# The second inverse step of a Fourier filter: three products in one PSUM bank

## The chip, the cores and the metric

The kernel runs on one core of a Trainium2 chip. The metric is the device time of one execution in microseconds (us). A core has TensorE (matrix products, which land in PSUM, here 8 banks of 128 partitions by 512 float32 columns), VectorE, ScalarE and GpSimd (elementwise work), and SyncE, whose queue issues most DMA transfers. In profile rows they are PE (PEld for its weight loads), DVE, ACT, POOL and SP. No GpSimd operation of this kernel touches PSUM.

## The reference

A signal `x` of 8 batches by 3008 positions by 256 channels is filtered in the frequency domain along its positions, and every position's 256 results then go through an MLP with a Gelu in its sigmoid form:

```
X = np.fft.rfft(x, axis=1)
y = np.fft.irfft(X * (filt_r + 1j * filt_i), n=3008, axis=1)
h = y.reshape(24064, 256) @ w_in          # 256 -> 2048
out = (h / (1 + np.exp(-1.702 * h))) @ w_out   # 2048 -> 256
```

All arrays are float32.

## The kernel before

**The transform.** 3008 = 64 x 47, so the transform of a batch is a 64-point one (first step), then a 47-point one (second forward step), the product with the filter, the 47-point inverse (second inverse step) and the 64-point inverse (first inverse step). Each is a matrix product with a table. The 64 frequencies of the first step are handled in 16 groups; a group has real and imaginary parts of two frequencies by 256 channels. The 47 positions are folded into 48 rows (sums of cosines and of sines), so the tables of the second steps are 48 by 48.

**High and low parts.** TensorE's fast float32 form (float32r) keeps fewer bits, so a value is split: the high part is a copy in float32r, the low part is the value less its high part. A product of two values is then high x high + high x low + low x high; the fourth, low x low, is small.

**The second steps of batch 1 on** (`fft`, lines 673 to 788). In group `i`, `forward(i)` (746) has its data from DRAM in the buffer `zy`: partitions 0 to 47 hold the high parts, 64 to 111 the low parts, real and imaginary part side by side. `second` (735) issues two products of 112 rows by 512 columns, one for the real and one for the imaginary part, each into a PSUM bank of its own. Its table `de_sb` stacks the high table under both the high and the low rows, and the low table beside it in other columns; so 48 rows of the bank receive high table x (high + low), and 48 other rows low table x (high + low). `halves` (666) adds the two: for each bank ScalarE copies 48 rows out, and VectorE adds the other 48 rows to them. In group 0 each of the two products is done as two of 256 columns, since one frequency has another table. `product` (657) multiplies with the filter: three VectorE operations into `u_buf` and `c_buf`, and an add on GpSimd. Then the result, 112 partitions with the real part in 0 to 47 and the imaginary part in 64 to 111, is split for the inverse step: for each part VectorE casts the 48 high rows into `zy`, and GpSimd subtracts them for the 48 low rows, which are put at the other part's partitions. `backward(i)` (764) runs `second` and `halves` once more, with the inverse table and with a tile `raw` as the end, and every other group stores to DRAM (`b_d`), from where `pair_signal` loads it for the first inverse step.

**The MLP.** Batch 0 is transformed first and its MLP runs in plain form, while batch 1 is transformed beside it; this part is ordered by the tile framework. From batch 1 on the MLP takes tokens in pairs of tiles of 512 and hidden units in pairs of blocks, with seven products for eight (`product_of`, `gelu`, `second_of`): 168 cycles of 45 matmuls of 512 columns (448 in a batch's last tile), with some six VectorE additions and subtractions a cycle. Beside the cycles of batch `b` runs the transform of batch `b + 1`, for `b` from 1 to 6; beside those of batch 7 there is none.

**What sets the order.** In this second part all operations are first recorded by `Planner` (189 on) and not issued. `add` notes for each the operations it must follow, by the boxes of the tiles that it reads and writes; `price` gives it a cost; `dues` a due time, backwards from a timeline of TensorE's work; and `plan` places them on the engines one after another, the most urgent first. It takes VectorE operations without PSUM and GpSimd operations one at a time. The order it finds is the order in which each engine executes: on every engine an operation waits until all those written ahead of it have started. `fft` is a generator, taken further by `advance` (1108) as the MLP's products are recorded: a transform's second steps are spread over the stretch that the MLP leaves. Banks of PSUM are given out by the planner as well: four (`bank_h`) serve the MLP's first products and the transform together, four (`bank_o`) the MLP's results.

The planner issues everything at one line, so in profile rows the planned part stands under L393, and the first part under L406. There operations are told apart by the tiles that they write and read. `bank_h<-zy,de_sb` are the products of both second steps, `raw<-bank_h,raw` of 48 partitions is the add of `halves` in the inverse step, and `c_buf<-bank_h,c_buf` is that in the forward step. Buffers of one pool can carry several names: `c_f` is the sum that feeds one of the MLP's four Gelus.

Of the kernel before, what the change touches and what calls it, by code (L numbers as in the profile page):

```python
# [9 lines left out]
F32 = mybir.dt.float32  # L10
# [4 lines left out]
ALU = mybir.AluOpType  # L15
# [170 lines left out]
class Planner:  # L186
# [56 lines left out]
    def add(self, eng, call, args, kw):  # L243
        o = Op()
        o.eng, o.call, o.args, o.kw = eng, call, args, kw
        aps = [a for a in (*args, *kw.values()) if isinstance(a, (bass.AP, View))]
        o.cost, o.extra, o.port = self.price(eng, call, args, aps)
        o.preds, o.succs, o.opens = set(), [], []
        o.names = {a.tensor.name: a.tensor for a in aps}
        n = len(self.ops)  # L250
        self.ops.append(o)
        for i, a in enumerate(aps):
            name, box, writes = a.tensor.name, self.box(a), i == 0
            if name not in self.seen:
                self.seen[name] = []
                if isinstance(a, View):
                    o.opens.append(a.tensor)
            kept = []
            for m, b, w in self.seen[name]:
                meets = b[0] < box[1] and box[0] < b[1] and b[2] < box[3] and box[2] < b[3]  # L260
                if meets and (w or writes) and m != n:
                    o.preds.add(m)
                inside = box[0] <= b[0] and b[1] <= box[1] and box[2] <= b[2] and b[3] <= box[3]
                if not (writes and inside and m != n):
                    kept.append((m, b, w))
            kept.append((n, box, writes))
            self.seen[name] = kept
        for name in o.names:
            self.users.setdefault(name, []).append(n)
# [142 lines left out]
def tile_kernel(  # L412
# [27 lines left out]
    def held(name, tag="f", shape=(P, 2, D)):  # L440

        if nc.on:
            return nc.tile("h", shape, F32, name, tag)
        return ps_h.tile(list(shape), F32, tag="h", name=name)
# [10 lines left out]

    tab = const.tile([P, sum(WIDTHS.values())], F32, tag="tab", name="tab")
    t1_sb = const.tile([P, 2, P], F32R, name="t1_sb")
    de_sb = const.tile([Q, 2, 4, Q], F32R, name="de_sb")
    HALF = NFC // 2
    table, at = {}, 0  # L460
    for name, w in WIDTHS.items():
# [97 lines left out]
    def split_de():  # L559

        pin = tc.keep_in_program_order
        de_f = table["de"].rearrange("p (m c) -> p m c", m=4)
        pin(nc.scalar.copy(t1_sb[:, 0], table["t1"]))
        pin(nc.vector.tensor_tensor(t1_sb[:, 1], table["t1"], t1_sb[:, 0].bitcast(F32), ALU.subtract))
        pin(nc.gpsimd.memset(de_sb.bitcast(F32), 0.0))
        for k in range(2):
            h, o = slice(64 * k, 64 * k + 48), slice(64 - 64 * k, 112 - 64 * k)
            pin(nc.scalar.copy(de_sb[h, k, :, h], de_f[h, :, h]))  # L570
            pin(nc.vector.tensor_tensor(de_sb[h, k, :, o], de_f[h, :, h], de_sb[h, k, :, h].bitcast(F32), ALU.subtract))
            pin(nc.gpsimd.tensor_copy(de_sb[o, k], de_sb[h, k].bitcast(F32)))

    def first_fft():

# [87 lines left out]
        nc.vector.tensor_tensor(u1, xs[:Q], f_r, ALU.mult)  # L663
        nc.gpsimd.tensor_tensor(u1, u1, u2, ALU.add)

    def halves(ps, dst):

        for k in range(2):
            h, o = slice(64 * k, 64 * k + 48), slice(64 - 64 * k, 112 - 64 * k)
            nc.scalar.copy(dst[h], ps[k][o])  # L670
            nc.vector.tensor_tensor(dst[h], ps[k][h], dst[h], ALU.add)

    def fft(b):

        a_d = dram.tile([2, 48, 64, D], F32, tag="a_d", name=f"a_d{b}")
        store = nc.sync if nc.on else nc.scalar
        xrs, split = {}, {}

        def load_x(c):
            if c < 6:  # L680
                xrs[c] = raw(f"x_{b}_{c}", "x")
                load_in(xrs[c], x[b, c])

        def parts(n):
            if n < 12:
                c, u = divmod(n, 2)
                xh, xl = half(f"xh_{b}_{c}_{u}"), half(f"xl_{b}_{c}_{u}")
                src = xrs[c][:, 2 * u : 2 * u + 2, :]
                nc.scalar.copy(xh, src)
                nc.gpsimd.tensor_tensor(xl, src, xh.bitcast(F32), ALU.subtract)  # L690
                split[n] = xh, xl

        load_x(0)
        if nc.on:
            load_x(1)
            yield 4.0
            parts(0)
            yield 2.0
        for c in range(6):
            if nc.on:  # L700
                ah, al = (nc.tile("ab", (P, 4, D), F32R, f"a{n}_{b}_{c}") for n in "hl")
            else:
                ah, al = (sb.tile([P, 4, D], F32R, tag="raw", name=f"a{n}_{b}_{c}", bufs=7) for n in "hl")
            for u in range(2):
                parts(2 * c + u + nc.on)
                xh, xl = split.pop(2 * c + u)
                ps = held(f"s1_{b}_{c}_{u}")
                mm3(ps, t1_sb[:, 0], t1_sb[:, 1], xh, xl)
                su = slice(2 * u, 2 * u + 2)
                nc.scalar.copy(ah[:, su], ps)  # L710
                nc.vector.tensor_tensor(al[:, su], ps, ah[:, su].bitcast(F32), ALU.subtract)
                yield 1.5
            load_x(c + 1 + nc.on)
            for j in range(2):
                n = NH * j + 4 * c
                for k, a in enumerate((ah, al)):
                    store.dma_start(
                        a_d[k, n : n + 4].rearrange("n k d -> k n d"), a[64 * j : 64 * j + 64].bitcast(F32)
                    )

        b_d = dram.tile([48, 64, D], F32, tag="b_d", name=f"b_d{b}")

        def load(i):
            for k in range(2):
                src = a_d[k].rearrange("n (k s) d -> n k s d", k=2)[:, :, 2 * i : 2 * i + 2, :]
                (nc.sync if nc.on else nc.gpsimd).dma_start(
                    zy[0][64 * k : 64 * k + 48, i % 2].rearrange("p k s d -> p k (s d)").bitcast(F32 if nc.on else F32R),
                    src.rearrange("n k s d -> n k (s d)"),
                )

        def load_f(i):
            for k in range(2):
                load_in(f_buf[64 * k : 64 * k + 48, 2 * (i % 2) : 2 * (i % 2) + 2], fs[:, 2 * i : 2 * i + 2])

        def second(i, m, src, name):

            ps = [held(f"{name}_{b}_{i}_{k}") for k in range(2)]
            for k in range(2):
                if i == 0:
                    nc.tensor.matmul(ps[k][:Q, 0], de_sb[:, k, m + 1], src[:, k, 0], start=True, stop=True)  # L740
                    nc.tensor.matmul(ps[k][:Q, 1], de_sb[:, k, m], src[:, k, 1], start=True, stop=True)
                else:
                    nc.tensor.matmul(ps[k][:Q], de_sb[:, k, m], src[:, k], start=True, stop=True)
            return ps

        def forward(i):

            ps = second(i, 0, zy[0][:Q, i % 2], "s2")
            if i + 2 < 16:
                load(i + 2)  # L750
            u1 = c_buf[i % 3]
            halves(ps, u1)
            product(i, u1, u1, f_buf[:, 2 * (i % 2) : 2 * (i % 2) + 2])
            y = zy[0][:, 2 + i % 2]
            for k in range(2):
                h, o = slice(64 * k, 64 * k + 48), slice(64 - 64 * k, 112 - 64 * k)
                nc.vector.tensor_copy(y[h, k], u1[h])
                nc.gpsimd.tensor_tensor(y[o, k], u1[h], y[h, k].bitcast(F32), ALU.subtract)
            if i + 2 < 16:
                load_f(i + 2)  # L760

        bes = {}

        def backward(i):
            g, u = divmod(i, 2)
            if u == 0:
                bes[g] = raw(f"b_{b}_{g}", "ab")
            ps = second(i, 2, zy[0][:Q, 2 + i % 2], "i2")
            halves(ps, bes[g][:Q, 2 * u : 2 * u + 2, :])
            if u == 1:  # L770
                be = bes.pop(g)
                for k in range(2):
                    (nc.sync if nc.on else nc.scalar).dma_start(b_d[:, 32 * k + 4 * g : 32 * k + 4 * g + 4, :], be[64 * k : 64 * k + 48])

        for i in range(2):
            load(i)
            load_f(i)

        for i in range(2):
            yield 5.0  # L780
        for i in range(17):
            if i < 16:
                forward(i)
                yield 3.3
            if i:
                backward(i - 1)
                yield 3.3
        b_of[b] = b_d
# [425 lines left out]
```

## Time and profile before

| | us |
|---|---|
| median of 3 runs | 2452.57 (2451.43 to 2454.61) |
| profiled execution, its own time | 2448.9 |
| its span, first to last instruction | 2447.1 |
| mean granted TensorE clock | 0.989 of full |

The page of the profile gives each engine's busy time and share of the span, and then the chain of work that ended last. Views by stretch give, for each stretch of time, the busy us of every engine with its number of instructions. A matmul's end is modelled, and matmuls overlap: a row's mean of 390 ns for one of 512 columns is not the time between two. What an engine waited for is told by "[idle before <-releaser]": how long it stood still, and whose end let it go on.

### The profile page before, as it was taken

The page shows a single profiled execution, that of the slowest core. Times are in us where ns is not written, and L with a number is a line of the kernel's source. Part 1 is how long each engine was busy: PE and PEld are TensorE (multiplying, and loading weights), DVE is VectorE, ACT ScalarE, POOL GpSimd, SP SyncE. Part 2 cuts the span into 40 slices and gives each one's busy share as a digit, 9 for nine tenths or more (in the row PEclk, how much of TensorE's full clock was granted, in tenths as well). Part 3 has the DMA queues.
Part 4 walks back from the last instruction along what each step waited for, and adds up shares of the span by engine and source line. Part 5 has one row for each costly group of instructions (what it writes and reads, how often), then busy time and mean ns, then how long its engine had stood idle before and what let it go on. Part 6 is the DMA issues. An engine that isn't in the chain of part 4 may idle for free.

```text
span 2447.1 us, 32185 instructions
## 1 busy us (share of the span) xinstructions
PE 2333.3 (95%) x10578; PEld 1897.0 (78%) x10578; DVE 1751.6 (72%) x2603; ACT 1615.3 (66%) x2937; POOL 1105.8 (45%) x789
## 2 busy tenths in 40 slices
PE   8789889989999999999999999999999999999999
PEld 6667668868788787887778777887778887888887
DVE  6776996578965889559985588756997588854443
ACT  5555554767767677667676677666776777766665
POOL 4654662445534445345543445444553455532111
PEclk9899999999999999999999999999999999999999
DMA  9455443777769777697677976778776886754443
GB/s 290 145 155 141 111 131 119 253 222 213 220 190 294 217 209 214 199 300 210 195 218 224 266 214 198 215 253 233 216 219 199 263 245 204 214 186 154 153 159 120
DMA packets 199191, 500.48 MB, mean 205 GB/s; under 512 B 21488, under 2 KB 94448, under 8 KB 199024
## 3 DMA queue, kind: packets, MB, share of 16 engines
q1 hardware_dynamic: 187456, 481.90, 64.6%
q10 hardware_dynamic: 7984, 10.23, 1.5%
q0 software_dynamic: 3584, 6.29, 1.3%
q8 instruction: 84, 1.38, 0.2%
q14 instruction: 83, 0.68, 0.1%
HBM read 392.95 MB, written 105.38 MB: 204 GB/s over the span
## 4 chain that ended last, share of the span: by engine, by line
PE 76%; DVE 15%; DMA 3%; issue 2%; ACT 2%; POOL 1%; SPq 0%; ACTq 0%; DVEq 0%; POOLq 0%
PE bank_h L393 38%; PE bank_o L393 33%; PE h L406 2%; PE o L406 2%; DVE c_buf L393 1%; DVE u_buf L393 1%; DVE gl L406 1%; DVE wb L393 1%; DVE c_buf L406 1%; DVE u_buf L406 1%; DVE w_tu L406 1%; DVE bank_h L393 1%; DVE zy L393 1%; DVE ws L406 1%; DVE gl L393 1%
## 5 line engine op out<-in xcount | busy, mean ns | idle before, releaser
L393 PE MATMUL bank_o<-wc 128*128 128x512 f32 (+1 forms) x2016 | 553.8, 390 | 5.4 <-ACT wc L393 3.5
L393 PE MATMUL bank_h<-y_a,wa 128*128 128x512 f32 (+1 forms) x1584 | 434.9, 393 | 14.8 <-DVE c_f L393 8.8
L393 PEld LDWEIGHTS bank_o<-wc 128*128 128x128 f32 x2016 | 378.2, 189 | 91.0 <-ACT wc L393 10.6
L393 POOL TENSOR_TENSOR wc<-c_f,wc 128x512 fp32r<-128x512 f32 (+1 forms) x168 | 214.0, 1274 | 495.6 <-ACT c_f L393 366.5
L393 PE MATMUL bank_o<-gh,wc 128*128 128x512 f32 (+1 forms) x1344 | 390.2, 388 | 0.5 <-ACT gh L393 0.2
L393 PEld LDWEIGHTS bank_h<-y_a,wa 128*128 128x128 f32 x1584 | 294.0, 189 | 85.1 <-DVE c_f L393 11.8
L393 POOL TENSOR_TENSOR zy<-c_buf,zy 48x512 fp32r<-48x512 f32 x192 | 273.7, 1426 | 132.1 <-DVE zy L393 116.4
L393 DVE TENSOR_TENSOR gl<-bank_h,gh 128x512 fp32r<-128x512 f32 (+1 forms) x336 | 226.8, 677 | 114.5 <-ACT bank_h L393 109.4
L393 ACT ACTIVATE bank_h<-bank_h 128x512 f32<-128x512 f32 (+1 forms) x504 | 297.8, 591 | 0.0
L393 PEld LDWEIGHTS bank_o<-gh,wc 128*128 128x128 f32 x1344 | 251.8, 188 | 49.2 <-ACT gh L393 2.6
L393 ACT COPY wb<-bank_h 128x512 f32<-128x512 f32 (+1 forms) x309 | 178.6, 578 | 161.8 <-PE bank_h L393 159.3
L393 PE MATMUL bank_h<-y_bt,wa 128*128 128x512 f32 (+1 forms) x960 | 272.1, 393 | 13.3 <-DVE c_f L393 10.0
L393 POOL TENSOR_TENSOR c_buf<-c_buf,u_buf 112x512 f32<-112x512 f32 x96 | 125.1, 1303 | 285.4 <-DVE c_buf L393 273.1
L393 ACT ACTIVATE gh<-bank_h 128x512 fp32r<-128x512 f32 (+1 forms) x336 | 197.4, 588 | 67.2 <-DVE bank_h L393 37.6
L393 DVE TENSOR_TENSOR raw<-bank_h,raw 48x512 f32<-48x512 f32 (+1 forms) x264 | 180.8, 687 | 63.0 <-ACT raw L393 55.2
L393 DVE TENSOR_TENSOR bank_h<-bank_h,g 128x512 f32<-128x512 f32 x224 | 155.8, 696 | 93.3 <-PE bank_h L393 50.6
L393 PEld LDWEIGHTS bank_h<-y_bt,wa 128*128 128x128 f32 x960 | 177.9, 189 | 54.6 <-DVE c_f L393 13.5
L393 PE MATMUL bank_o<-gl,wc 128*128 128x512 f32 (+1 forms) x672 | 217.0, 387 | 0.0
L393 ACT COPY g<-bank_h 128x512 f32<-128x512 f32 x224 | 131.8, 588 | 111.0 <-PE bank_h L393 103.5
L393 DVE TENSOR_TENSOR wc<-bank_h,wc 128x512 fp32r<-128x512 f32 x168 | 115.7, 689 | 109.8 <-ACT bank_h L393 108.9
L393 DVE TENSOR_TENSOR c_f<-bank_h,wb 128x512 f32<-128x512 f32 (+1 forms) x168 | 112.2, 668 | 78.7 <-ACT wb L393 76.2
L393 PE MATMUL bank_h<-zy,de_sb 112*112 112x512 f32 (+1 forms) x408 | 154.6, 392 | 10.6 <-DVE wc L393 6.4
(166 smaller groups left out, 4154.5 us busy)
## 6 DMA issues: line engine op xcount, KB each, us to landing
wa<-w SPq DMA_DIRECT2D x168, 896.0 KB, 7.0
wc<-w SPq DMA_DIRECT2D x168, 512.0 KB, 4.3
f_buf<-fs SPq DMA_DIRECT2D x224, 192.0 KB, 3.9
a_d<-raw SPq DMA_DIRECT2D x144, 256.0 KB, 5.2
zy<-a_d SPq DMA_DIRECT2D x192, 192.0 KB, 4.3
out_dram<-out SPq DMA_DIRECT2D x40, 512.0 KB, 6.1
raw<-in_x_dram SPq DMA_DIRECT2D x36, 512.0 KB, 6.3
b_d<-raw SPq DMA_DIRECT2D x96, 192.0 KB, 3.9
```

Of the source, the lines that this page charges most:

```text
L393: getattr(getattr(self.nc, o.eng), o.call)(*map(real, o.args), **{k: real(v) for k, v in o.kw.items()})
L406: return real(*args, **kw)
```

## The change

The second inverse step of batches 1 to 7 is computed in another way. After the filter, VectorE casts all 112 rows into the first half of a `zy` buffer in one operation, and GpSimd subtracts all 112 rows for the low parts into the second half. The inverse table is a tile of its own, `e_sb`, with a high and a low part, each 112 by 112 with the real and the imaginary table on its diagonal. `backward` issues three products of 112 rows by 512 columns (high x high, high x low, low x high) which add up in one PSUM bank; in group 0 it is three for each of the two frequencies, of 256 columns. One ScalarE copy of 112 rows takes the sum to `raw`. The product of the low parts is no longer formed there. The forward step keeps its products and its `halves`, now written out inside `forward`, with a table `d_sb` half the size of `de_sb`. In the planner, a write of TensorE counts as one of the whole bank.

```
@@ Planner.add
+            if eng == "tensor" and writes:
+                box = (0, P, 0, 2048)
@@ tables
-    de_sb = const.tile([Q, 2, 4, Q], F32R, name="de_sb")
+    d_sb = const.tile([Q, 2, 2, Q], F32R, name="d_sb")
+    e_sb = const.tile([Q, 2, 2, Q], F32R, name="e_sb")
@@ split_de
-        pin(nc.gpsimd.memset(de_sb.bitcast(F32), 0.0))
+        pin(nc.scalar.copy(e_sb[:, 0], de_f[:Q, 2:4]))
+        pin(nc.vector.tensor_tensor(e_sb[:, 1], de_f[:Q, 2:4], e_sb[:, 0].bitcast(F32), ALU.subtract))
+        pin(nc.gpsimd.memset(d_sb.bitcast(F32), 0.0))
         for k in range(2):
...
@@ forward: the split for the inverse step
-            y = zy[0][:, 2 + i % 2]
-            for k in range(2):
-                h, o = slice(64 * k, 64 * k + 48), slice(64 - 64 * k, 112 - 64 * k)
-                nc.vector.tensor_copy(y[h, k], u1[h])
-                nc.gpsimd.tensor_tensor(y[o, k], u1[h], y[h, k].bitcast(F32), ALU.subtract)
+            y = zy[0][:Q, 2 + i % 2]
+            nc.vector.tensor_copy(y[:, 0], u1)
+            nc.gpsimd.tensor_tensor(y[:, 1], u1, y[:, 0].bitcast(F32), ALU.subtract)
@@ backward
-            ps = second(i, 2, zy[0][:Q, 2 + i % 2], "i2")
-            halves(ps, bes[g][:Q, 2 * u : 2 * u + 2, :])
+            ps, y = held(f"i2_{b}_{i}"), zy[0][:Q, 2 + i % 2]
+            for to, m, of in [(0, 1, 0), (1, 0, 1)] if i == 0 else [(slice(0, 2), 0, slice(0, 2))]:
+                for n, (wk, yk) in enumerate(((0, 0), (0, 1), (1, 0))):
+                    nc.tensor.matmul(ps[:Q, to], e_sb[:, wk, m], y[:, yk, of], start=n == 0, stop=n == 2)
+            nc.scalar.copy(bes[g][:Q, 2 * u : 2 * u + 2, :], ps[:Q])
```

## Rows read from the trace of the kernel before

**Rows 1.** The page, parts 1 and 4: engines' busy time; the chain that ended last.
```profile
PE 2333.3 (95%) x10578; PEld 1897.0 (78%) x10578; DVE 1751.6 (72%) x2603; ACT 1615.3 (66%) x2937; POOL 1105.8 (45%) x789
...
PE 76%; DVE 15%; DMA 3%; issue 2%; ACT 2%; POOL 1%; SPq 0%; ACTq 0%; DVEq 0%; POOLq 0%
```

**Rows 2.** Busy us (and instructions) by stretch: from:to, length, engines, clock, DMA; second-step stretches.
```profile
502.00:705.00 203.00, 193.17 (x840) 152.28 (x841) 170.18 (x257) 142.31 (x257) 97.91 (x71) 1.00 0.70 207
790.00:993.00 203.00, 193.37 (x850) 154.02 (x849) 170.34 (x257) 141.89 (x256) 100.33 (x71) 1.00 0.73 211
1082.00:1287.00 205.00, 195.71 (x854) 155.86 (x853) 170.75 (x257) 142.51 (x258) 100.83 (x71) 0.99 0.72 209
1376.00:1582.00 206.00, 196.76 (x852) 156.51 (x851) 170.71 (x257) 142.32 (x257) 100.72 (x71) 0.98 0.72 209
1671.00:1876.00 205.00, 195.79 (x853) 155.69 (x852) 170.58 (x257) 142.37 (x257) 100.73 (x71) 0.99 0.72 209
1953.00:2159.00 206.00, 203.02 (x906) 164.91 (x905) 173.39 (x269) 150.43 (x270) 104.58 (x74) 1.00 0.73 218
sum 1228.00, PE 1177.82 PEld 939.26 DVE 1025.95 ACT 861.83 POOL 605.10; mean PE 196.30 PEld 156.54 DVE 170.99 ACT 143.64 POOL 100.85
```

**Rows 3.** The same view, the sum of the five strips between those stretches.
```profile
sum 429.00, PE 428.29 PEld 364.26 DVE 231.43 ACT 297.64 POOL 186.85; mean PE 85.66 PEld 72.85 DVE 46.29 ACT 59.53 POOL 37.37
```

**Rows 4.** The same view: batch 1's second steps, and the MLP alone at the end.
```profile
150.00:420.00 270.00, 241.98 (x1078) 191.85 (x1078) 206.40 (x290) 142.86 (x262) 136.96 (x114) 0.99 0.50 138
2200.00:2400.00 200.00, 200.00 (x918) 167.56 (x918) 87.96 (x134) 121.95 (x221) 40.94 (x28) 1.00 0.44 157
```

**Rows 5.** TensorE's matmuls in order of time (start, us, operation): two runs of six.
```profile
2307.04 1.52 PE L393 MATMUL bank_h<-y_bt,wa 128*128 128x512 f32 x6
2308.40 1.52 PE L393 MATMUL bank_o<-wc 128*128 128x512 f32 x6
```

**Rows 6.** Waits of TensorE, its largest: us in total, times, longest.
```profile
PE bank_h L393 <- DVE c_f L393: 18.8, 12, 3.5
```

**Rows 7.** All engines in order of time, around TensorE's longest wait.
```profile
1398.45 3.20 POOL L393 TENSOR_TENSOR zy<-c_buf,zy 48x512 fp32r<-48x512 f32 x2 [1.07 <-DVE zy L393]
...
1398.86 1.67 DVE L393 SCALAR_TENSOR_TENSOR u_buf<-c_buf,f_buf 48x512 f32<-48x512 f32 x1
...
1400.56 1.64 DVE L393 TENSOR_TENSOR u_buf<-c_buf,f_buf 48x512 f32<-48x512 f32 x1
...
1403.58 1.65 PE L393 MATMUL bank_h<-y_bt,wa 128*128 128x512 f32 x3 [3.52 <-DVE c_f L393]
```

**Rows 8.** One tile's instructions, `u_buf`: ns shortest/median/longest, first and last start.
```profile
L393 DVE SCALAR_TENSOR_TENSOR u_buf<-c_buf,f_buf x96: 678/687/1719, 519.4 to 2139.7; 48x512 f32<-48x512 f32 x96
```

**Rows 9.** TensorE in order of time: a lone product of the second steps among others.
```profile
2101.68 0.40 PE L393 MATMUL bank_h<-zy,de_sb 112*112 112x512 f32 x1
2101.92 0.87 PE L393 MATMUL bank_o<-gh,wc 128*128 128x512 f32 x3
```

**Rows 10.** VectorE's groups, 500 to 2200 us: count, busy us, mean ns, idle before.
```profile
L393 DVE TENSOR_TENSOR raw<-bank_h,raw 48x512 f32<-48x512 f32 x192 | 131.7, 686 | 23.9 <-ACT raw L393 20.4 <-DMA f_buf<-fs 0.3
L393 DVE CAST zy<-c_buf 48x512 fp32r<-48x512 f32 x192 | 85.6, 446 | 4.6 <-POOL c_buf L393 1.1
...
L393 DVE TENSOR_TENSOR c_buf<-c_buf,f_buf 112x512 f32<-112x512 f32 x96 | 69.8, 727 | 2.6
```

**Rows 11.** GpSimd's groups of the second steps, the same stretch and columns.
```profile
L393 POOL TENSOR_TENSOR zy<-c_buf,zy 48x512 fp32r<-48x512 f32 x192 | 273.7, 1426 | 132.1 <-DVE zy L393 116.4 <-PE bank_h L393 7.3 <-PE bank_o L393 1.6
L393 POOL TENSOR_TENSOR c_buf<-c_buf,u_buf 112x512 f32<-112x512 f32 x96 | 125.1, 1303 | 285.4 <-DVE c_buf L393 273.1 <-PE bank_h L393 12.2
```

**Rows 12.** ScalarE's copies out of PSUM, the same stretch and columns.
```profile
L393 ACT COPY raw<-bank_h 48x512 f32<-48x512 f32 x192 | 111.7, 582 | 48.0 <-PE bank_h L393 42.3 <-DMA f_buf<-fs 1.0
...
L393 ACT COPY g<-bank_h 128x512 f32<-128x512 f32 x186 | 109.4, 588 | 97.0 <-PE bank_h L393 90.2 <-DVE c_buf L393 1.9 <-DVE bank_h L393 1.2
```

**Rows 13.** One tile's instructions, `de_sb`: its clearing (ns, start).
```profile
L406 POOL MEMSET de_sb<- x1: 858/858/858, 132.9 to 132.9; 112x896 f32 x1
```

More of the change, by code (lines that the diff above doesn't have):

```diff
@@ L566, in split_de @@
         pin(nc.vector.tensor_tensor(t1_sb[:, 1], table["t1"], t1_sb[:, 0].bitcast(F32), ALU.subtract))
-        pin(nc.gpsimd.memset(de_sb.bitcast(F32), 0.0))
+        pin(nc.scalar.copy(e_sb[:, 0], de_f[:Q, 2:4]))
+        pin(nc.vector.tensor_tensor(e_sb[:, 1], de_f[:Q, 2:4], e_sb[:, 0].bitcast(F32), ALU.subtract))
+        pin(nc.gpsimd.memset(d_sb.bitcast(F32), 0.0))
         for k in range(2):
             h, o = slice(64 * k, 64 * k + 48), slice(64 - 64 * k, 112 - 64 * k)
-            pin(nc.scalar.copy(de_sb[h, k, :, h], de_f[h, :, h]))
-            pin(nc.vector.tensor_tensor(de_sb[h, k, :, o], de_f[h, :, h], de_sb[h, k, :, h].bitcast(F32), ALU.subtract))
-            pin(nc.gpsimd.tensor_copy(de_sb[o, k], de_sb[h, k].bitcast(F32)))
+            pin(nc.scalar.copy(d_sb[h, k, :, h], de_f[h, 0:2, h]))
+            pin(nc.vector.tensor_tensor(d_sb[h, k, :, o], de_f[h, 0:2, h], d_sb[h, k, :, h].bitcast(F32), ALU.subtract))
+            pin(nc.gpsimd.tensor_copy(d_sb[o, k], d_sb[h, k].bitcast(F32)))
     def first_fft():
@@ L664, in product @@
         nc.gpsimd.tensor_tensor(u1, u1, u2, ALU.add)
-    def halves(ps, dst):
-        for k in range(2):
-            h, o = slice(64 * k, 64 * k + 48), slice(64 - 64 * k, 112 - 64 * k)
-            nc.scalar.copy(dst[h], ps[k][o])
-            nc.vector.tensor_tensor(dst[h], ps[k][h], dst[h], ALU.add)
     def fft(b):
@@ L733, in load_f, with forward @@
                 load_in(f_buf[64 * k : 64 * k + 48, 2 * (i % 2) : 2 * (i % 2) + 2], fs[:, 2 * i : 2 * i + 2])
-        def second(i, m, src, name):
-            ps = [held(f"{name}_{b}_{i}_{k}") for k in range(2)]
+        def forward(i):
+            ps = [held(f"s2_{b}_{i}_{k}") for k in range(2)]
+            src, u1 = zy[0][:Q, i % 2], c_buf[i % 3]
             for k in range(2):
                 if i == 0:
-                    nc.tensor.matmul(ps[k][:Q, 0], de_sb[:, k, m + 1], src[:, k, 0], start=True, stop=True)
-                    nc.tensor.matmul(ps[k][:Q, 1], de_sb[:, k, m], src[:, k, 1], start=True, stop=True)
-                else:
[L743 to L748, printed above, removed]
+                    nc.tensor.matmul(ps[k][:Q, 0], d_sb[:, k, 1], src[:, k, 0], start=True, stop=True)
+                    nc.tensor.matmul(ps[k][:Q, 1], d_sb[:, k, 0], src[:, k, 1], start=True, stop=True)
+                else:
+                    nc.tensor.matmul(ps[k][:Q], d_sb[:, k, 0], src[:, k], start=True, stop=True)
             if i + 2 < 16:
                 load(i + 2)
-            u1 = c_buf[i % 3]
-            halves(ps, u1)
-            product(i, u1, u1, f_buf[:, 2 * (i % 2) : 2 * (i % 2) + 2])
-            y = zy[0][:, 2 + i % 2]
             for k in range(2):
                 h, o = slice(64 * k, 64 * k + 48), slice(64 - 64 * k, 112 - 64 * k)
-                nc.vector.tensor_copy(y[h, k], u1[h])
-                nc.gpsimd.tensor_tensor(y[o, k], u1[h], y[h, k].bitcast(F32), ALU.subtract)
+                nc.scalar.copy(u1[h], ps[k][o])
+                nc.vector.tensor_tensor(u1[h], ps[k][h], u1[h], ALU.add)
+            product(i, u1, u1, f_buf[:, 2 * (i % 2) : 2 * (i % 2) + 2])
+            y = zy[0][:Q, 2 + i % 2]
+            nc.vector.tensor_copy(y[:, 0], u1)
+            nc.gpsimd.tensor_tensor(y[:, 1], u1, y[:, 0].bitcast(F32), ALU.subtract)
             if i + 2 < 16:
```

## The prediction

> **What bounds the kernel now.** I read the page first. TensorE is busy for 95% of the span and carries 76% of the chain that ended last; VectorE carries 15% of that chain [rows 1]. So one engine bounds most of it, but not all. Which stretches belong to the other part is told by the busy time by stretch. The second-step stretches (each from some 15 us ahead of a batch's first product with `de_sb` to some 10 us behind its last) are six, 1228 us in all; TensorE is busy 1177.8 us of them and VectorE 1026.0 us, 84% [rows 2]. In the five strips between them VectorE is busy 54% and TensorE 428.3 of 429 us [rows 3]. At the end, where no transform runs beside the MLP, TensorE is busy 200 of 200 us and VectorE 44% [rows 4]. TensorE loses time only where VectorE is at its fullest.
>
> How much it loses can't be read from busy time, because a matmul's modelled 0.39 us overlaps the next one: six that follow each other take 1.36 us, 0.2267 us each [rows 5]. I count instead. The undisturbed stretch runs 918 matmuls in 200 us, 0.2179 us each over its mix of 512, 448 and 128 columns [rows 4]. At that rate the six stretches with 840, 850, 854, 852, 853 and 906 matmuls would take 183.0, 185.2, 186.1, 185.6, 185.9 and 197.4 us, and they took 203, 203, 205, 206, 205 and 206 [rows 2]. So they lose 20.0, 17.8, 18.9, 20.4, 19.1 and 8.6 us: 104.8 us. (The mix is a little poorer in 128-column ones here; I put that at nothing.)
>
> The rows show TensorE 95.9% busy in the six stretches, 50 us idle [rows 2]. The Trainium skill ("Perfetto Trace Analysis", section Identifying the Most-Contended Engine) says that matmul busy time misjudges the headroom, and that the busy share of weight loads judges it better. By it: weight loads 939.3 of 1228 us, 76.5%, against 167.6 of 200, 83.8%, where nothing stalls, so 8.7% or 107 us lost; the trace bears the rule out. By the busy rows half of 50 us would come back and pay for the added products with 3 us to spare, no measurable change; by the rule the sum below stands.
>
> Who makes TensorE wait? Its largest wait is on VectorE's `c_f` add, 18.8 us in 12 waits, the longest 3.5 us [rows 6]. That longest one in order of time: GpSimd runs its two `zy` subtractions for 3.20 us from 1398.45; beside them two VectorE `u_buf` products take 1.67 and 1.64 us where the median is 0.69; behind them in VectorE's queue stands the `c_f` add, and TensorE, released by it, starts again at 1403.58 after 3.52 us [rows 7, 8]. Half of the cause is the length of VectorE's queue, half is that it slows beside GpSimd.
>
> **The change, part by part** (a step is one of 16 groups; 7 batches have them, batch 1 in the first, automatically ordered part, 6 in the planned part, so 96 planned steps).
>
> *TensorE, added.* The inverse step issues three products of 512 columns for two (six of 256 for four in group 0). In a run of like ones a product takes 0.2267 us [rows 5]; a lone `de_sb` product takes 0.24 us to the next start [rows 9]. Three in a row are nearer the run: 96 x 0.2267 = 21.8 us (23.0 by 0.24). It lies on the bound engine and nothing hides it. In batch 1 it is 16 x 0.2267 = 3.6 us; there TensorE is busy only 242.0 of 270 us [rows 4], so I take 0, between +3.6 and, with relief like that below, -8.
>
> *VectorE, removed.* Two adds of 48x512 per step, 131.7 us, and one of two casts, half of 85.6 us [rows 10]: 174.5 us, 29.1 per stretch. That the remaining cast of 112x512 costs what a 48x512 one did, I take from the filter's products: 0.727 us on average over 112 rows [rows 10], 0.687 at the median over 48 [rows 8], so partitions cost nothing. VectorE's load in the six stretches goes from 1026 to 851 us, 71% of 1197 us.
>
> *GpSimd, removed.* Two subtractions of 1.426 us become one of 112x512, as its add at 1.303: 273.7 - 96 x 1.303 = 148.6 us [rows 11]. The other half of the stall above shrinks with it, and the low part, which TensorE needs, is there one subtraction earlier.
>
> *ScalarE.* Two copies of 48x512, 111.7 us, become 96 of 112x512, near the 128x512 copy's 0.588: 56.4 [rows 12]. ScalarE isn't what TensorE waits for most; I count nothing.
>
> *PSUM.* The inverse step holds one of four banks where it held two, from the first product to one copy, not to a copy and an add. That can only free banks sooner; not priced apart from the stalls.
>
> *Edits priced at nothing.* The planner's full-bank box orders matmuls of one bank that TensorE runs in order anyway. But planned order and due times are worked out anew, and every written order shifts; the rows can't price that, and its bounds are those of the stalls below. The tables' split: the 0.858 us clear of `de_sb` halves, and one ScalarE copy and one VectorE subtraction come in. It is done once, around 133 us [rows 13], ahead of batch 1's second steps in the stretch from 150 us on [rows 4]; within 1 us either way, hidden by what lies between.
>
> *What comes back.* All 104.8 us is the ceiling, nothing the floor. The only stretch that shows what such a stretch can do with the same steps is the sixth, which loses 8.6 us [rows 2]; its VectorE load, 84%, is above the 71% to come. I let all six end there: 6 x 8.6 = 51.6 us stay, 53.2 us come back. What is late next: ScalarE's Gelu inputs and the copies before them, which wait for TensorE itself.
>
> **Sum.** The profiled execution took 2448.9 us (span 2447.1). 2448.9 + 21.8 - 53.2 = 2417.5. The median of the runs shown, 2452.57, is 3.7 above that execution: 2421.
>
> **Rivals.**
> *A: slower.* The stalls belong to the written order, not to VectorE's load: an operation in VectorE's queue ahead of the add that TensorE wants, as `c_f` was. A new order has new places of that kind. For it: the 3.52 us wait had three VectorE operations of the transform ahead of one of the MLP [rows 7], and that is an order. Against: the strips with VectorE at 54% lose nothing under the same planner. Price: the added 21.8 to 25.4 us with nothing given back: 2474 to 2478. It decides from below 22 to 25 of 105 us returned, about a fifth to a quarter.
> *B: even.* The wait moves to ScalarE or GpSimd, and about a fourth returns: 17 to 27 us, 2448 to 2457.
> *C: nearly all returns.* VectorE was simply the bound in the stretches, as its 84% beside TensorE's loss suggests, and at 71% they run like the strips. Full return gives 2448.9 + 21.8 - 104.8 + 3.7 = 2370; 80% returns: 2391. Against: the sixth stretch still loses 8.6, and a written order never fits exactly.
> That the change does not do what it says (the products don't run, or run elsewhere) has nothing for it in the rows, and I give it no chance.
>
> **How the numbers follow.** Forecast, 2395 to 2437: 0.55. C, below 2395: 0.08. Between 2437 and 2464: 0.19, of which 0.09 lie within 0.2% (2447.7 to 2457.5; 0.2% is about what a measurement of this kernel can tell from no change), 0.05 below and 0.05 above. A, above 2464: 0.18, for the new order can also cost more than it did. So faster 0.55 + 0.08 + 0.05 = 0.68, same 0.09, slower 0.05 + 0.18 = 0.23. The range leaves out 2 in 10: 2390 (most of C) to 2468 (the far part of A).
>
> **What would show it.** Right: 48x512 adds into `raw` gone from VectorE; one 112x512 copy of about 0.59 us on ScalarE and one `zy` subtraction of about 1.3 us on GpSimd per step, 96 each; three products a step some 0.23 us apart; VectorE near 71% in the stretches, each some 5 us shorter; the strips unchanged; no wait of 3.5 us on `c_f`. Wrong: VectorE's load falls by the 29 us a stretch and TensorE still loses 18 us in each (A), or new waits of like size on ScalarE or GpSimd (B), or stretches at 0.218 us a matmul (C); or strips and batch 1 change by more than a few us, which I took to be untouched.

## The result, and the profile after

| | before | after |
|---|---|---|
| median, us | 2452.52 (2451.43 to 2454.61, 4 runs) | 2393.13 (2391.09 to 2394.11, 4 runs) |
| profiled execution, its span | 2448.9, 2447.1 | 2393.86, 2391.9 |

The ratio is 0.9756, 95% interval 0.9739 to 0.9773: 59.4 us faster, and about twice the 31.5 us that was forecast. It lies inside the stated range of 2390 to 2468, but below the forecast's own band (2395 to 2437), where the prediction put rival C with a chance of 0.08. In the profiled executions the span falls by 55.2 us. The page after, part 1 (engines' busy time) and part 4 (the chain that ended last):

```profile
PE 2324.2 (97%) x10697; PEld 1922.4 (80%) x10697; DVE 1554.8 (65%) x2268; ACT 1539.9 (64%) x2826; POOL 939.0 (39%) x677
...
PE 84%; DVE 6%; DMA 5%; issue 2%; ACT 2%; POOL 1%; SPq 0%; ACTq 0%; DVEq 0%
```

Beside [rows 1] VectorE has 196.8 us less and its part of the chain falls from 15% to 6%. The six second-step stretches after, by the same rule (15 us ahead of the first product, 10 us behind the last; columns as in [rows 2]), and then the sum of the five strips between them:

```profile
475.00:666.00 191.00, 186.96 (x836) 152.12 (x835) 136.85 (x205) 127.73 (x235) 75.79 (x55) 1.00 0.74 219
755.00:949.00 194.00, 190.64 (x856) 156.17 (x855) 142.20 (x208) 130.61 (x239) 76.38 (x55) 1.00 0.72 219
1043.00:1237.00 194.00, 190.64 (x856) 156.29 (x855) 141.33 (x207) 130.51 (x240) 75.48 (x55) 1.00 0.74 220
1331.00:1526.00 195.00, 191.48 (x851) 156.37 (x850) 140.88 (x206) 129.31 (x237) 74.56 (x55) 0.99 0.72 217
1622.00:1817.00 195.00, 189.95 (x843) 155.06 (x842) 140.30 (x205) 128.47 (x235) 73.46 (x54) 0.99 0.74 217
1899.00:2102.00 203.00, 201.74 (x909) 165.79 (x908) 146.89 (x219) 138.40 (x252) 79.93 (x58) 1.00 0.74 219
sum 1172.00, PE 1151.41 PEld 941.80 DVE 848.46 ACT 785.03 POOL 455.60; mean PE 191.90 PEld 156.97 DVE 141.41 ACT 130.84 POOL 75.93
```

```profile
sum 455.00, PE 450.10 PEld 382.52 DVE 248.43 ACT 309.24 POOL 193.09; mean PE 90.02 PEld 76.50 DVE 49.69 ACT 61.85 POOL 38.62
```

The count of the prediction on these rows: 5151 matmuls at the 0.2179 us of [rows 4] are 1122.4 us, and the stretches took 1172: 49.6 us lost, where before it was 104.8 and the forecast left 51.6. VectorE is busy 72% (forecast 71%). The count takes every matmul alike; by columns (488 a matmul on average in these stretches, 481 in the undisturbed one, from the groups of matmuls by shape) the losses are 89 and 34 us, with the same difference. Weight loads say it without a count: 941.8 of 1172 us is 80.4%, against 83.8% where nothing stalls, 4.1% or 48 us lost. That is one of the measures by which the Trainium skill ("Perfetto Trace Analysis", section Identifying the Most-Contended Engine) judges TensorE's headroom; the trace agrees again. The strips, by busy time, lose 4.9 us where they lost 0.7 [rows 3]; they are 455 us long and no longer 429, because some of the MLP's products moved there out of the stretches, and so each stretch is 9.3 us shorter on average and not 5.

So the planned part is 55.2 shorter by stalls, 21.8 longer by products and 4.2 longer in the strips: 29.2 us shorter in all, where the forecast had 31.4. The other 26 us of the span lie in the first part, nearly all of them in batch 1's second steps. Its stretch, from the first to the last of its products, before and then after (same columns):

```profile
216.00:389.00 173.00, 148.55 (x637) 112.94 (x637) 158.13 (x223) 90.12 (x161) 104.48 (x89) 0.99 0.41 105
```

```profile
214.00:369.00 155.00, 150.74 (x674) 121.13 (x675) 124.61 (x179) 84.03 (x153) 85.50 (x74) 0.99 0.46 120
```

TensorE's largest waits there, before and then after (214 to 390 us; total, times, longest):

```profile
PE o L406 <- DVE gl L406: 10.0, 11, 2.9
```

```profile
PE o L408 <- DVE gl L408: 2.3, 1, 2.3
```

Before, VectorE was busy 158.13 of 173 us, 91%, more than in any planned stretch, and TensorE lost 173 - 637 x 0.2179 = 34.2 us in this one stretch; after it is 80%, and 155 - 674 x 0.2179 = 8.1 us. All of TensorE's waits that the view lists there come to 23.5 us before, 22.0 of them on VectorE, and to 4.6 after; the largest is on `gl`, a subtraction of the MLP. 26.1 us came back, and 3.6 were paid for products: 22.5 of the 26. The last 3.5 lie elsewhere in the first part, and no row is shown for them.

The long wait of [rows 7] is still there, shorter. The same place of the same batch after, all engines in order of time:

```profile
1352.73 0.69 DVE L395 SCALAR_TENSOR_TENSOR u_buf<-c_buf,f_buf 48x512 f32<-48x512 f32 x1
1352.78 1.80 POOL L395 TENSOR_TENSOR zy<-c_buf,zy 112x512 fp32r<-112x512 f32 x1 [1.08 <-DVE zy L395]
...
1353.45 1.67 DVE L395 TENSOR_TENSOR u_buf<-c_buf,f_buf 48x512 f32<-48x512 f32 x1
...
1355.76 0.68 DVE L395 TENSOR_TENSOR c_f<-bank_h,wb 128x512 f32<-128x512 f32 x1
...
1356.50 0.96 PE L395 MATMUL bank_h<-y_bt,wa 128*128 128x512 f32 x3 [2.11 <-DVE c_f L395]
```

GpSimd has one subtraction of 1.80 us where it had two in 3.20, one of VectorE's two `u_buf` products is slowed and not both (the first, 0.69 us, starts 0.05 us ahead of GpSimd's operation; the second starts behind it), and TensorE waits 2.11 us, not 3.52. After, TensorE's largest waits in the planned part are these (470 to 2110 us; total, times, longest):

```profile
PE bank_h L395 <- ACT wb L395: 8.7, 11, 1.2
PE bank_h L395 <- DVE c_f L395: 7.9, 4, 2.1
```

ScalarE has taken the first place; VectorE's `c_f` was 18.8 us in 12 waits [rows 6].

### The profile page after: what moved, and what is told of

The parts are those of the page before. It is cut to its first block, busy times and chain, and to the rows that moved or that the text cites. A ratio compares the mean times of both kernels' runs of the same rounds, so it can differ in the third digit from the quotient of the medians.

```text
span 2391.9 us, 31593 instructions
## 1 busy us (share of the span) xinstructions
PE 2324.2 (97%) x10697; PEld 1922.4 (80%) x10697; DVE 1554.8 (65%) x2268; ACT 1539.9 (64%) x2826; POOL 939.0 (39%) x677
## 4 chain that ended last, share of the span: by engine, by line
PE 84%; DVE 6%; DMA 5%; issue 2%; ACT 2%; POOL 1%; SPq 0%; ACTq 0%; DVEq 0%
PE bank_h L395 40%; PE bank_o L395 34%; PE h L408 4%; PE o L408 4%; PE i L408 1%; DMA wa<-w 1%; DVE w_tu L408 1%; DVE gl L408 1%; PE s L408 1%; DMA zy<-a_d 1%; DVE u_buf L395 1%; DMA x<-in_x_dram 1%; DVE c_buf L395 1%; DMA wb<-b_d 1%; DVE bank_h L395 1%
## 5 line engine op out<-in xcount | busy, mean ns | idle before, releaser
L395 PE MATMUL bank_o<-wc 128*128 128x512 f32 (+1 forms) x2016 | 528.0, 387 | 0.4 <-DMA wc<-w 0.3
L395 PE MATMUL bank_h<-y_a,wa 128*128 128x512 f32 (+1 forms) x1584 | 423.3, 391 | 11.9 <-DVE c_f L395 3.7
L395 PE MATMUL bank_o<-gl,wc 128*128 128x512 f32 (+1 forms) x672 | 210.8, 388 | 0.0
L395 DVE TENSOR_TENSOR c_buf<-bank_h,c_buf 48x512 f32<-48x512 f32 x192 | 132.1, 688 | 75.7 <-ACT c_buf L395 72.6
L395 ACT COPY c_buf<-bank_h 48x512 f32<-48x512 f32 x192 | 111.5, 581 | 93.4 <-PE bank_h L395 88.8
L395 POOL TENSOR_TENSOR zy<-c_buf,zy 112x512 fp32r<-112x512 f32 x96 | 133.7, 1393 | 73.4 <-DVE zy L395 71.0
```

The lines of the kernel that those rows point to most:

```text
L395: getattr(getattr(self.nc, o.eng), o.call)(*map(real, o.args), **{k: real(v) for k, v in o.kw.items()})
```

## Experiments

All are timed against before on the same chip. The median of before itself was 2454.3 us for e1 to e4, 2450.4 for e5 to e8 and 2452.5 for e9 to e12, so a difference of two medians out of different groups is good to some 4 us; the ratios and the spans are the better measure. "Span of the six" is the time from the first forward product of the planned part to the last inverse one, which the view by tile gives (first and last start; 516.9 and 2149.3 us before, so 1632.4; 490.2 and 2092.3 after, so 1602.1). "Lost, batch 1" is counted over its stretch as above, the six half-width products of a group taken as three.

| kernel | median, us | ratio to before (95%) | span of the six | batch 1: VectorE, lost |
|---|---|---|---|---|
| before | 2452.5 | | 1632.4 | 91%, 34.2 |
| after | 2393.1 | 0.9756 (0.9739 to 0.9773) | 1602.1 | 80%, 8.1 |
| e1 batch 1 only | 2426.7 | 0.9887 (0.9865 to 0.9909) | 1632.4 | 81%, 8.0 |
| e2 planned part only | 2416.8 | 0.9853 (0.9834 to 0.9873) | 1597.8 | 91%, 34.4 |
| e3 two banks | 2403.2 | 0.9793 (0.9771 to 0.9815) | 1606.8 | 78%, 9.0 |
| e4 two products | 2371.4 | 0.9671 (0.9653 to 0.9688) | 1580.4 | 81%, 9.1 |
| e5 adds back | 2411.8 | 0.9840 (0.9825 to 0.9855) | 1606.9 | 85%, 19.1 |
| e6 before, with the box | 2450.3 | 0.9998 (0.9988 to 1.0008) | 1632.3 | 91%, 35.0 |
| e7 copy on VectorE | 2408.4 | 0.9831 (0.9816 to 0.9846) | 1605.1 | 83%, 16.1 |
| e8 split twice | 2417.8 | 0.9860 (0.9845 to 0.9875) | 1604.5 | 86%, 24.4 |
| e9 adds and split | 2442.0 | 0.9960 (0.9945 to 0.9974) | 1631.3 | 86%, 35.6 |
| e10 all back | 2462.9 | 1.0045 (1.0030 to 1.0061) | 1644.5 | 88%, 36.3 |
| e11 other order | 2394.9 | 0.9754 (0.9732 to 0.9775) | 1602.9 | 81%, 7.6 |
| e12 cast on ScalarE | 2390.6 | 0.9745 (0.9729 to 0.9761) | 1594.1 | 74%, 14.0 |

**The change in one part alone, e1 and e2.** Both forms of the inverse step stand side by side (the old one with a table `i_sb`), and the part decides; e2 has the condition the other way:

```
+            if not nc.on:                      # e2: if nc.on
                 ...                            # new split / new products, copy
+            else:
+                ...                            # old split / old products, halves
```

> The new inverse step in batch 1 alone (the automatically ordered part); batches 2 to 7 keep the old split, the two stacked products and the halves. The trace of after shows the first part 26 us shorter (planned part starts at 404.0 us, before at 429.9). My theory: that gain belongs to the change itself, whose VectorE and GpSimd relief also works there: 2452.5 - 26 = 2426 us. Rival: the first part's gain is an accident of how the whole program was ordered, and comes and goes with any edit: 2447 to 2458 us, or a first part whose length lies anywhere between.

> The new inverse step in batches 2 to 7 alone (the planned part); batch 1 keeps the old one. My theory: this is the sum of the prediction, 96 x 0.2267 us more of TensorE and some 53 us of stalls given back, so about 2421 to 2424 us, with the first part as long as before (planned part from about 430 us). Rival (the planned part needs the earlier start, or the two parts are not additive): more than 8 us away from that.

e1 is 27.6 us below before, e2 37.5. Together 65 us, with intervals of about 5 us each, so they add up to the change's 59.4. In e1 the span of the six is what it was before to a tenth of a us, and batch 1's loss is that of after; in e2 it is the reverse. The first part's gain is the change's own, and it is where the forecast was short. e2 lies 4 us below what was expected of it, 2421 to 2424.

**Two banks, e3.**

```
-            ps, y = held(f"i2_{b}_{i}"), zy[0][:Q, 2 + i % 2]
+            pss, y = [held(f"i2_{b}_{i}_{k}") for k in range(2)], zy[0][:Q, 2 + i % 2]
...                                             # frequency k into pss[k], 3 products of 256 columns
+                nc.scalar.copy(bes[g][:Q, 2 * u + k, :], pss[k][:Q, 0])
```

> After, but the two frequencies of a group in PSUM banks of their own: six products of 256 columns for three of 512, two ScalarE copies of 112x256 for one of 112x512; VectorE and GpSimd as in after. Tells the banks from the load. If the single bank is what gave TensorE its time back (rival), two banks take most of the 81 us of stalls away again: 2430 us or more. If it is VectorE's and GpSimd's load (my theory): only the shorter passes cost, 6 x 0.12 for 3 x 0.227 us and a second ScalarE access of about 0.2 us a group: 2394 to 2402 us.

10 us slower than after by the medians, just above what my theory allowed, far below what the bank would have cost as the cause. The planned part grew by 4.7 us, near the 3.8 of the half-width passes (96 x 0.04), and batch 1 lost 0.9 us more. The trace is of the fastest of the four executions (2396.6 us), so it shows no more than 3 of the 10 us; what the others lost isn't shown. A second bank, held until a copy, is not what cost the time. Before, the two were held until VectorE's add; this run doesn't test that.

**Two products, e4.**

```
-                for n, (wk, yk) in enumerate(((0, 0), (0, 1), (1, 0))):
+                for n, (wk, yk) in enumerate(((0, 0), (0, 1))):
```

> After without the product low table x high values: it leaves out that part of the result's low bits. TensorE has two products a group as before the change. My theory: after the change TensorE is the bound in the stretches, so a product fewer gives its full 0.2267 us, 112 x 0.2267 = 25 us: 2366 to 2370 us. Rival: the stretches still wait for other engines, and the product runs in idle time: 2383 us or more.

21.7 us below after by the medians, and the planned span is shorter by 21.7 us: 96 x 0.2267 = 21.8. In the planned part a product is paid in full, to the tenth; TensorE is the bound there. The median is 1.4 us above the expected 2366 to 2370, which counted batch 1's 16 groups in. There it isn't settled: batch 1's stretch is 3.0 us shorter (152 us, 9.1 lost, against 155 and 8.1), but it begins 2.6 us later, and the planned part starts where it did (490.4 against 490.2). This kernel is the fastest run, but it does not compute the same: the low part of the inverse table is left out.

**The adds back, and the split back, e5 and e8.**

```
 e5: behind the copy to dst = bes[g][:Q, 2 * u : 2 * u + 2, :]
+            for k in range(2):
+                h = slice(64 * k, 64 * k + 48)
+                nc.vector.tensor_tensor(dst[h], ps[h], dst[h], ALU.max)
 e8:
-            nc.vector.tensor_copy(y[:, 0], u1)
-            nc.gpsimd.tensor_tensor(y[:, 1], u1, y[:, 0].bitcast(F32), ALU.subtract)
+            for k in range(2):
+                h = slice(64 * k, 64 * k + 48)
+                nc.vector.tensor_copy(y[h, 0], u1[h])
+                nc.gpsimd.tensor_tensor(y[h, 1], u1[h], y[h, 0].bitcast(F32), ALU.subtract)
```

> After, with the two VectorE operations of 48x512 out of PSUM put back behind the copy in the inverse step (each takes the larger of the sum and its own copy, so the values stay). TensorE, the split and the number of banks are those of after; the one bank is held until VectorE is done. If VectorE's load is what cost TensorE its time (my theory), the 1.38 us a group are three quarters of what was taken away, and more than half of the 81 us comes back as stalls: 2435 to 2460 us, with batch 1's stretch longer again by 10 us or more. If the single accumulated product or the shorter way of the low part did it: below 2410 us.

> After, with the split for the inverse step done as two casts on VectorE and two subtractions on GpSimd of 48 rows each, as before; the products, the bank and the copy are those of after. Tells the split from the adds. By VectorE's load alone (0.43 us a group, a quarter of what was taken off): 2400 to 2413 us. If GpSimd's second subtraction, which slows VectorE beside it and delays the low part, is half of the cause, as the prediction had it: 2420 us or more. If it is hidden: within 4 us of after.

e5 misses: 2411.8 us, not 2435 or more. Three quarters of VectorE's work came back, and the planned span grew by 4.8 us; the first part took 13.9 (504.1 against 490.2), 11.0 of it in batch 1's loss. e8 lies between its expectations, above the 2413 of VectorE's load alone and below the 2420 of GpSimd as half of the cause; it adds 2.4 us to the planned span and 16.3 to batch 1's loss. In batch 1's stretch VectorE has 16 casts more than after and is busy some 25 us longer, 12 of them in the MLP's `gl` subtractions, which e8 doesn't touch (1195 ns on average for 933). Before, with as many subtractions on GpSimd, they took 862, so how much VectorE is slowed there hangs on the order too. Batch 1's stretch and a planned one, of e5 and then of e8:

```profile
217.00:383.00 166.00, 154.50 (x674) 122.86 (x675) 140.54 (x208) 84.72 (x153) 84.72 (x74) 0.97 0.43 112
1353.00:1550.00 197.00, 191.39 (x848) 155.93 (x848) 154.12 (x237) 129.50 (x236) 72.47 (x54) 0.99 0.72 216
```

```profile
220.00:393.00 173.00, 157.77 (x682) 125.46 (x681) 149.45 (x195) 84.79 (x155) 108.10 (x90) 0.96 0.41 108
1356.00:1553.00 197.00, 192.23 (x856) 157.22 (x855) 148.09 (x224) 129.74 (x238) 100.24 (x71) 0.99 0.74 216
```

The planned stretch has VectorE at 78% and 75%, above the 72% after, and TensorE loses 12.2 and 10.5 us, where after loses 9.6 in the same stretch and before 20.3. A loss in proportion to VectorE's load, which e5's expectation rested on, is refuted for the planned part.

**Both back, and all back, e9 and e10.** e9 is e5 and e8 in one. e10 has e8's split, two banks as e3, and behind each copy of 112x256 two operations of 48x256 like those of e5.

> After, with both put back: the two VectorE operations of 48x512 behind the copy, and the split in two casts and two subtractions of 48 rows. Alone, the first cost the planned part 3.4 us of lost TensorE time and the second 2.3. If VectorE's load works as a threshold (my theory now: 92 to 94% busy in before's stretches, 88% and 84% with one half put back), both together bring it over 90% and the planned part loses 20 to 35 us more than after; with batch 1's part, some 22 us, that is 2435 to 2450 us. If the effects just add up (rival): 6 us more in the planned part, and 2420 to 2436 us in all.

> After, with everything put back that the change took from the other engines, but the three products kept: two banks a group (a frequency each, products of 256 columns), two copies of 112x256, four VectorE operations of 48x256, and the split in two casts and two subtractions. If load and banks are the whole of it, TensorE loses again what it lost before the change, and the added products come on top: 2470 to 2485 us. If the old form itself (stacked parts, a later low part) cost the time: below 2460 us.

e9 is as its expectation had it for a threshold. Where the two halves cost the planned span 4.8 and 2.4 us alone, together they cost 29.2 (1631.3 less 1602.1): not a sum. From the first forward product to the end of the span it is 3.9, 2.3 and 25.1, and by the count of matmuls over all six stretches 6.5, 9.1 and 30.8, so the excess is certain and its size is not. In batch 1 they do add up: 11.0 and 16.3 alone, 27.5 together. But not all of that is waiting. TensorE's granted clock in batch 1's stretch is 0.93 of full in e9, against 0.99 before and after: 0.06 of 182 us is some 11 us. It is 0.96 in e8, 0.97 in e5 (some 5 and 3 us) and 0.98 in e12. The clock falls from the higher level, 2.4 GHz, to the lower, 1.2, after TensorE stood still; e9, TensorE alone, columns as above (busy, clock):

```profile
278.00:280.00 2.00, 0.00 (x0) 1.00 0.00 0
282.00:284.00 2.00, 0.91 (x4) 0.50 0.78 145
284.00:286.00 2.00, 2.00 (x9) 0.50 0.00 0
286.00:288.00 2.00, 2.00 (x7) 0.50 0.91 225
292.00:294.00 2.00, 2.00 (x11) 1.00 0.51 121
```

TensorE's wait of 3.18 us on VectorE's `gl` ends at 280.84, one of 1.52 us on ScalarE at 283.09; from 282 to 288 the clock is 0.50. These waits cost more than their length. The first and last products of e9's planned part (ns, then first and last start), and its stretches: batch 1's, a planned one and the sixth:

```profile
L395 PE MATMUL bank_h<-zy,e_sb x306: 276/395/483, 528.7 to 2151.0; 112*112 112x512 f32 x135, 112*112 112x256 f32 x18
L395 PE MATMUL bank_h<-zy,d_sb x204: 274/399/628, 519.7 to 2139.8; 112*112 112x512 f32 x90, 112*112 112x256 f32 x12
```

```profile
216.00:398.00 182.00, 161.41 (x672) 126.77 (x673) 155.72 (x223) 83.76 (x151) 106.12 (x90) 0.93 0.38 99
1381.00:1586.00 205.00, 197.40 (x870) 159.14 (x869) 167.92 (x255) 130.94 (x238) 97.08 (x70) 0.99 0.68 208
1953.00:2161.00 208.00, 206.23 (x926) 168.96 (x925) 178.67 (x269) 139.79 (x255) 105.42 (x74) 1.00 0.72 217
```

VectorE is at 82% of the planned stretch, 83% in the one of before [rows 2], and TensorE loses 15.4 us. The sixth stretch doesn't fit a threshold in VectorE's share alone: with 86% in e9 and 84% before [rows 2] it has the highest shares and the smallest losses, 6.2 and 8.6 us. What differs there stays open. The shares that the expectations of e9 (92 to 94, 88 and 84%) and e12 (81 and 84%; ScalarE 75 and 58%) name are higher than the rows give: 83 to 84% before, 78 and 75% with one half back, 72 and 80% after (ScalarE 66 and 54%). Their order is the same.

e10 misses: 2462.9 us, between the two expectations. Its planned stretch, with VectorE at 84%:

```profile
1388.00:1594.00 206.00, 198.80 (x910) 161.24 (x910) 172.08 (x288) 133.10 (x257) 98.22 (x71) 0.98 0.69 208
```

Against before, its planned part has 25.6 us more of products (96 groups, 6 x 0.12 for 2 x 0.2267), and its span is only 12.1 longer, so 13.5 us of before's stalls are still missing. Of the 52.1 us that the planned part got back (30.3 of span and 21.8 of paid products) some 38.6 are explained by what e10 put back; the rest lies in something that it doesn't, such as the old form's stacked parts or its two longer copies, and stays open. e10 has 13.2 us more of span than e9, of which products are 3.8; the rest comes with the second bank, now held until VectorE has read it, and with VectorE's shorter and more numerous operations. The two weren't told apart.

**The planner alone, e6 and e11.** e6 is before with the two lines of the full-bank box. e11 is after with

```
-    HOP, REACH, NEAR = 0.2, 30.0, 2.5
+    HOP, REACH, NEAR = 0.25, 30.0, 2.5
```

> Before, with the planner's full-bank box alone. I priced it at nothing: within 4 us of before. Rival (the new order of everything, not the load, made the gain): a move of 10 us or more either way.

> After, with the same work and the planner's allowance between engines at 0.25 us for 0.2, so that the planned part is written in another order (the first part stays). It shows what the order by itself is worth: if the gain hung on one lucky order, 2405 us or more; if it belongs to the load, within 6 us of after, 2388 to 2399 us.

Both as the load has it. In e6 the box alone gives another order of the old work (VectorE's operations follow each other otherwise from the first group on), with the span of before to a tenth of a us; in e11 another order of the new work has the same span within a us. The gain does not hang on one order.

**A move between engines, e7 and e12.** In e7 the copy out of the bank is `nc.vector.tensor_copy`, in e12 the split's cast is `nc.scalar.copy`; each is one word of the code.

> After, with the inverse step's one copy of 112x512 out of PSUM on VectorE (about 0.69 us) and not on ScalarE (0.588). After, TensorE's largest wait in the planned part is on ScalarE (10.2 us), and VectorE is at some 70% of a stretch. If ScalarE is what is late now: 2380 to 2390 us. If VectorE's load still sets what TensorE loses (my theory, a third of what was taken off comes back): 2400 to 2415 us.

> After, with the cast of 112x512 in the split on ScalarE (about 0.6 us) and not on VectorE (0.42 to 0.6 us). ScalarE is at 75% in the planned stretches and 58% in batch 1's, VectorE at 81% and 84%. If VectorE's load still costs at that level: 2380 to 2389 us, most of it in batch 1's part. If it works as a threshold that is already passed: 2389 to 2395 us. If ScalarE, on which TensorE now waits most, is what is late: 2397 us or more.

e7 is slower by 15 us, as expected of VectorE's load, 3.0 of them in the planned span: batch 1 loses twice what it did. e12 is faster by 2.6, but its interval overlaps that of after, so a gain isn't shown. What it hides is two moves of opposite sign. The planned span falls by 8.0 us, and batch 1's stretch grows by 5:

```profile
215.00:375.00 160.00, 152.34 (x670) 121.42 (x671) 119.00 (x162) 92.14 (x168) 79.05 (x74) 0.98 0.45 118
1336.00:1531.00 195.00, 191.97 (x854) 157.05 (x853) 130.57 (x191) 138.54 (x255) 74.29 (x55) 0.99 0.73 217
```

VectorE is at its lowest in both, 74% and 67%, ScalarE at 58% and 71%, and yet batch 1 loses 14.0 us. The granted clock (0.98) is some 1.6 us of the 5.9 that this is more than after. So below some 80% VectorE's share no longer tells the loss in the automatically ordered part; why the cast on ScalarE hurts there wasn't tried. A version with that cast on ScalarE in the planned part alone would join the two better halves; no run shows it.

## Why the prediction was right, and where it fell short

The measured time is one that the prediction left to rival C, and C's mechanism is not what happened: the stretches still lose 49.6 us. The planned part came out as it was summed (29.2 us shorter, 31.4 forecast); batch 1, which the sum had at 0, brought the rest. That the time still fell inside the stated range is in part luck.

*TensorE's price.* Right: 21.8 us predicted for the planned part, and e4 takes 21.7 off by dropping one product. The three products follow each other as a run does; TensorE in order of time, after:

```profile
1403.68 0.87 PE L395 MATMUL bank_h<-zy,e_sb 112*112 112x512 f32 x3
1404.38 0.63 PE L395 MATMUL bank_o<-gh,wc 128*128 128x512 f32 x2
```

0.70 us for three, 0.233 each, between the 0.2267 and the 0.24 that were weighed.

*VectorE, GpSimd and ScalarE removed.* Right but for one term. Their groups in the planned part after:

```profile
L395 DVE CAST zy<-c_buf 112x512 fp32r<-112x512 f32 x96 | 57.7, 601 | 5.8 <-POOL c_buf L395 5.8
```

```profile
L395 POOL TENSOR_TENSOR zy<-c_buf,zy 112x512 fp32r<-112x512 f32 x96 | 133.7, 1393 | 73.4 <-DVE zy L395 71.0
```

```profile
L395 ACT COPY raw<-bank_h 112x512 f32<-112x512 f32 x96 | 56.5, 588 | 46.9 <-PE bank_h L395 45.2 <-DVE u_buf L395 0.3
```

The copy is 0.588 us as taken. The subtraction is 1.393, not 1.303: GpSimd gave back 140 us, not 148.6. The cast is 0.601 on average, not the 0.446 of [rows 10]: it gave back 27.9 us, not 42.8, and all of VectorE 159.6, not 174.5. That "partitions cost nothing" holds for a cast left alone, 0.41 us; what the mean has on top comes from GpSimd beside it (last section).

*What comes back in the planned part.* Right in size: 8.6 us a stretch were left in the forecast, 49.6 / 6 = 8.3 are left (4.9 in the sixth, 7.5 to 11.3 in the others). By columns the ceiling was 89 us and not 104.8: the mix of matmuls, put at nothing, was worth 15 us of it, but the same amount after, so the gain stands. The reason given was half right. Load on VectorE and GpSimd is the cause of about half of it by e9 (29.2 of 52.1 us) and of three quarters with what e10 adds; order is not (e6, e11), and a second bank that is held until a copy is not (e3). But the prediction made VectorE's queue and GpSimd's slowing one half of the cause each, and neither half put back alone (e5, e8) costs the planned part anything near half; only both together do.

*Batch 1.* This is the step that failed: "there TensorE is busy only 242.0 of 270 us [rows 4], so I take 0, between +3.6 and, with relief like that below, -8". It measured 26.1 us back in the stretch, and 27.6 (22 to 33) in e1 alone. The row that I read covers 150 to 420 us and has VectorE at 76% there; the stretch of the second steps is 216 to 389, and in it VectorE stood at 91% and TensorE lost 34.2 us, almost twice a planned stretch. I had counted matmuls for the six planned stretches and took busy time for this one: the very mistake that the prediction warns of in its second paragraph. Its own count on the row that it shows would have done: 270 - 1078 x 0.2179 = 35.1 us lost. With the count, the rule used for the other six (they end at 8.6) gives 34.2 - 8.6 = 25.6 us back for 3.6 us of products, and the forecast would have been 2399.

*The rivals.* A (stalls stay with the order) is refuted by the result, 55.2 us of stalls gone, and by e6 and e11; B (the wait moves) shows only as a trace, ScalarE's 8.7 us; C (all returns) is refuted by the 49.6 us left, although its time is the one that came. Of the signs that were to show the prediction wrong, one came true: batch 1 and the strips were taken to be untouched. Batch 1 is answered above; the strips were off by 4.2 us, which no run follows up.

## What to carry to other kernels

Add work to the bound engine if it takes more off an engine that makes it wait: 25 us of products bought some 81 us of stalls here. Count work at the rate of an undisturbed stretch, stage by stage and with the stage's own limits, before saying that a stage has nothing to give; VectorE's average over a wider window, and TensorE's busy time, hid the richest one. And a stall that comes from a nearly full engine can be cured by a part of the relief, so putting back one half and seeing no loss does not show that the half was idle: put back both.

## What was not expected of the hardware

VectorE's cast from SBUF to SBUF takes 0.41 us alone and up to 1.45 beside a GpSimd operation. All casts of the planned part after (ns shortest/median/longest), and then two of them in order of time:

```profile
L395 DVE CAST zy<-c_buf x96: 407/419/1451, 497.8 to 2087.1; 112x512 fp32r<-112x512 f32 x96
```

```profile
1352.29 0.41 DVE L395 CAST zy<-c_buf 112x512 fp32r<-112x512 f32 x1
...
1357.92 1.27 POOL L395 TENSOR_TENSOR wc<-c_f,wc 128x512 fp32r<-128x512 f32 x1 [0.71 <-ACT c_f L395]
...
1358.16 1.32 DVE L395 CAST zy<-c_buf 112x512 fp32r<-112x512 f32 x1
```

The second cast begins while GpSimd's subtraction runs and ends 0.29 us after it. So it goes throughout: of the 96 casts 35 begin while a GpSimd operation runs, and 34 of these end 0.27 to 0.29 us after that operation's end, however late it is; the other 61 take 0.41 to 0.43, three of them with a GpSimd operation that begins behind them. `u_buf` products do the same with 0.54 to 0.56 us (24 of the 26 that begin beside a GpSimd operation), as the one at 1353.45 above (to 1355.12, against 1354.58). So what such an operation loses is what is left of GpSimd's operation. The adds that read PSUM stay at 0.69 us throughout.

The Trainium skill ("GPSIMD Engine Reference", section Key points) says that GpSimd shares its SBUF interfaces with VectorE, in contention with VectorE operations of two SBUF inputs or in a two-port mode. The trace agrees for the `u_buf` products, which have two SBUF inputs (0.69 and 1.67 us). The cast has one; whether it runs in a two-port mode, no row shows. This is why a cast saved was worth less than its count, and why moving the split's subtractions matters beyond GpSimd's own time.
